# Row statistics of the late output projection: sums with the additions, squares and one normalising instruction on ScalarE, and the next phase's sums one unit ahead

## The chip, the cores and the metric

The kernel runs on one core of one Trainium2 chip. The metric is device time in microseconds (us) for one execution of the whole program, all four layers. One core has TensorE (PE, matmuls, with a separate record PEld for loading the stationary operand), VectorE (DVE), ScalarE (ACT), GpSimd (POOL) and SyncE (SP), which here issues every DMA. Each engine works through its own queue in order, so an instruction that waits holds up everything behind it on that engine.

## The reference

Four layers on an activation of 2048 rows by 640 columns, fp32. Layers 1 and 3 are attention over a sliding window of 256 with 32 heads of 20 columns; layers 2 and 4 are a Fourier mixing, written as products with DFT matrices. Each has a layer norm in front and a residual around it.

```python
x = x + _A_ref(_layernorm(x), A_wqkv, A_wo)
x = x + _B_ref(_layernorm(x), seq_re, seq_im, hid_re, hid_im)
x = x + _A_ref(_layernorm(x), A_wqkv, A_wo)
x = x + _B_ref(_layernorm(x), seq_re, seq_im, hid_re, hid_im)

def _layernorm(x, eps=1e-5):
    m = mean(x); v = var(x)
    return (x - m) / sqrt(v + eps)
```

`_A_ref` ends with a product by `wo` (the output projection). `_B_ref` is Re(DFT over the sequence of (DFT over the columns of x)). The change touches the place where these meet: the end of the output projection, its residual addition, the layer norm of the Fourier layer, and the beginning of the DFT over the sequence. This place occurs twice, in layers 1 to 2 and in layers 3 to 4. It is called the seam below, the first and the second.

## The kernel before

**Products.** fp32 operands are split into a high and a low part (`split`: the high part is a ScalarE copy, L156, the low part a subtraction on VectorE or GpSimd, L162), and a product is three matmuls (L169, L1139).

**Output projection.** The 640 columns that enter it are five chunks of 128. Three are multiplied early, during the heads; `late` multiplies the last two and adds the result to the early part, in 16 row blocks `t` of 128 rows. A row block is two halves of 320 columns with six matmuls each (L169), and each half ends in an addition on VectorE out of PSUM (L888) into the tile `xw`. After the heads these halves alternate between two PSUM banks, 5 and 6. The four sets of rows need their operands loaded and multiplied first (`load_o`, L741 on VectorE).

**Late rows, as they are now.** After the second addition VectorE takes the statistics of the row (`stats`: two BATCH_NORM_STATS, L183, an aggregate, L185, and the addition of epsilon, L187) and the negative mean (L894). The rest is posted: `post(d, f)` runs `f` after `d` ticks, and a tick passes for every `PACE` = 0.65 of accounted work (`spend`: 0.147 for a matmul of `late`, 2.7 for a unit a1, 1.4 for a2, 2.0 for b7). In ticks after the row's end: at 3 the power -0.5 on GpSimd (L896); at 5 the store of the row; at 6 two ScalarE instructions, x minus mean (L857) and times the power (L858). Rows of the first half (t below 8) are split at 8. Rows of the second half belong to row t-8: at 8 their columns 384 to 640 are added to those of row t-8 on GpSimd (`sum1`, L951), at 10 that sum is split. The last two rows take another way (`norm_last`, `norm_rest`): power at 1, VectorE normalises columns 384 to 640 (L869), adds (L951) and at 3 splits; the other columns follow at 8 on ScalarE (L876, L877).

**The DFT over the sequence** is a list of units (`take_fourier`): a1 for j = 0 to 7, a2 for j = 0 to 5, then b7 0, a2 6, b7 1, a2 7, b7 2, b5 0 to 2, b 3 to 7, and g 0 to 7. A unit (`seq`) loads matrices ahead (`load_to`, L1049), forms sums and differences of them and splits them (`cut_to`; L1062 on GpSimd, L1070 on VectorE), prepares its row operand (`x_to`) and then multiplies. While rows are left, `after_heads` runs about one unit after each row, and `unit` starts a2 j only when the split of row j+9 has been issued, a2 6 and a2 7 only after that of row 15.

**Row operands of the b units** (`x_to`): `xb3_to` splits a difference that GpSimd made (`sum3`, L955), `xb4_to` first calls `sum4_to`, two VectorE additions (L963, L964), and splits their result, and `parts` splits 128 columns of the row (the tile `rr`), which the unit's first matmuls read.

Of the kernel before, what the change touches and what calls it, by code (L numbers as in the profile page):

```python
# [15 lines left out]
P = 128  # L16
S = 2048
D = 640
# [5 lines left out]
NB = S // P  # L24
# [3 lines left out]
EPS = 1e-5  # L28
# [32 lines left out]
class Net:  # L61
# [114 lines left out]
            pass  # L176


    def stats(self, x, root=True):
        nc = self.nc  # L180
        st = self.ln.tile([P, 2, 6], F32, name="st", tag="st")
        for i in range(2):
            nc.vector.bn_stats(out=st[:, i, :], in_=x[:, i * 320:(i + 1) * 320])  # L183
        mv = self.ln.tile([P, 2], F32, name="mv", tag="mv")
        nc.vector.bn_aggr(out=mv, in_=st)  # L185
        rs = self.ln.tile([P, 2], F32, name="rs", tag="rs")
        nc.vector.tensor_scalar_add(rs[:, 0:1], mv[:, 1:2], EPS)  # L187
        if not root:
            return mv, rs
# [660 lines left out]
    def late(self, xsrc, xdst, hook):  # L850
        nc = self.nc
        ks = range(EARLY, KC)
        w = dict(zip(ks, self.late_w))

        def norm(t, xw, st, nm):
            xn = self.y_part(t)
            nc.scalar.activation(xn, xw, AF.Identity, bias=nm, scale=1.0)  # L857
            nc.scalar.activation(xn, xn, AF.Copy, scale=st[1][:, 1:2])  # L858
            if t < NB // 2:
                self.post(2, lambda: self.split_x(t, 0, 384))  # L860
            else:
                j = t - NB // 2
                self.post(2, lambda: self.sum1(j, nc.gpsimd))
                self.post(4, lambda: self.split_x(j, 384, 640))

        def norm_last(t, xw, st):

            xn, j = self.y_part(t), t - NB // 2
            nc.vector.tensor_scalar(out=xn[:, 384:], in0=xw[:, 384:], scalar1=st[0][:, 0:1], scalar2=st[1][:, 1:2],  # L869
                                    op0=OP.subtract, op1=OP.mult)  # L870
            self.sum1(j, nc.vector)
            self.post(1, lambda: self.split_x(j, 384, 640, nc.vector))

        def norm_rest(t, xw, st, nm):
            xn = self.y_part(t)
            nc.scalar.activation(xn[:, :384], xw[:, :384], AF.Identity, bias=nm, scale=1.0)  # L876
            nc.scalar.activation(xn[:, :384], xn[:, :384], AF.Copy, scale=st[1][:, 1:2])  # L877

        for t in range(NB):
            sb, i = t // 4, t % 4  # L880
            y = self.y_part(t)
            xw = self.raw()
            for hf in range(2):
# [4 lines left out]
                nc.vector.tensor_tensor(out=xw[:, cs], in0=p, in1=y[:, cs], op=OP.add)  # L888
                if hf == 0:
                    yield 1  # L890
            self.post(5, lambda t=t, xw=xw: nc.sync.dma_start(xdst[t * P:(t + 1) * P, :], xw))
            st = self.stats(xw, False)
            nm = self.ln.tile([P, 1], F32, name="nm", tag="nm")
            nc.vector.tensor_scalar_mul(nm, st[0][:, 0:1], -1.0)  # L894
            fast = t >= NB - 2
            self.post(1 if fast else 3, lambda st=st: nc.gpsimd.tensor_tensor(  # L896
                out=st[1][:, 1:2], in0=st[1][:, 0:1], in1=self.half, op=OP.pow))
            if NB // 2 - 1 <= t < NB - 1:
                self.post(4, lambda t=t: self.sum3(t - NB // 2 + 1))
            if fast:  # L900
                self.post(2, lambda t=t, xw=xw, st=st: norm_last(t, xw, st))
                self.post(8, lambda t=t, xw=xw, st=st, nm=nm: norm_rest(t, xw, st, nm))
            else:
                self.post(6, lambda t=t, xw=xw, st=st, nm=nm: norm(t, xw, st, nm))
            hook(t)
            self.late_t = t + 1
            yield 1
# [178 lines left out]
    def x_to(self, n):  # L1086
        nc = self.nc
        while self.n_x <= min(n, len(self.order) - 1):
            u = self.n_x
            self.n_x += 1  # L1090
            ph, j = self.order[u][2:]
            a, b = self.y_part(j), self.y_part(j + NB // 2)
            first = self.order[u][:2] == (0, 0)

            x = [self.xa[j]]
            if ph in ("b", "b7"):
                x = [self.xb[j], self.xm[j % 2]]
# [347 lines left out]
```

## Time and profile before

| | |
|---|---|
| median of 3 runs | 2337.34 us (2332.91 to 2339.71) |
| profiled execution, its own time | 2337.11 us |
| its span, first to last instruction | 2335.4 us |
| PE busy | 2245.9 us (96%) |
| DVE busy | 1576.0 us (67%) |
| ACT busy | 1110.4 us (48%) |
| POOL busy | 1010.4 us (43%) |

A span is the time from the first to the last instruction. Busy shares are averages over stages that have different limits; the two seams lie at about 574 to 700 us and 1733 to 1858 us, and the prediction reads them stage by stage. In rows of groups the figures are count, busy us, mean ns of one, then the engine's idle time in front of them and what ended it. In rows of waits they are total us, times, longest us. In rows of the timeline they are start, duration, engine, line, operation, and in brackets the idle time in front and its releaser. In rows of stages each engine has its busy us and number of instructions, and PEclk is the granted clock of TensorE as a share of full speed.

### The profile page before, as it was taken

The page shows a single profiled execution, that of the slowest core. Times are in us where ns is not written, and L with a number is a line of the kernel's source. Part 1 is how long each engine was busy: PE and PEld are TensorE (multiplying, and loading weights), DVE is VectorE, ACT ScalarE, POOL GpSimd, SP SyncE. Part 2 cuts the span into 40 slices and gives each one's busy share as a digit, 9 for nine tenths or more (in the row PEclk, how much of TensorE's full clock was granted, in tenths as well). Part 3 has the DMA queues.
Part 4 walks back from the last instruction along what each step waited for, and adds up shares of the span by engine and source line. Part 5 has one row for each costly group of instructions (what it writes and reads, how often), then busy time and mean ns, then how long its engine had stood idle before and what let it go on. Part 6 is the DMA issues. An engine that isn't in the chain of part 4 may idle for free.

```text
span 2335.4 us, 40458 instructions
## 1 busy us (share of the span) xinstructions
PE 2245.9 (96%) x13584; PEld 1679.5 (72%) x13584; DVE 1576.0 (67%) x3781; ACT 1110.4 (48%) x1875; POOL 1010.4 (43%) x1506
## 2 busy tenths in 40 slices
PE   8999999999979999999999999999998899999999
PEld 7964444456758888889999554445667688888899
DVE  6357677675888888872451677776758888788622
ACT  3125555655645555541331355556566555456310
POOL 3036665776845132340120466557677332242300
PEclk9999999999999999999999999999999899999999
DMA  5545555674535454655455455557735353536453
GB/s 190 172 133 170 169 166 162 207 210 143 190 101 163 140 175 142 213 174 165 162 163 178 138 167 164 159 182 207 213 127 183 104 167 131 185 123 229 162 165 101
DMA packets 217264, 385.02 MB, mean 165 GB/s; under 512 B 38880, under 2 KB 85472, under 8 KB 217056
## 3 DMA queue, kind: packets, MB, share of 16 engines
q1 hardware_dynamic: 217056, 382.43, 51.9%
q8 instruction: 108, 1.77, 0.3%
q14 instruction: 100, 0.82, 0.1%
HBM read 267.39 MB, written 113.77 MB: 163 GB/s over the span
## 4 chain that ended last, share of the span: by engine, by line
PE 39%; ACT 3%; POOL 3%; DVE 3%; DMA 1%; issue 1%; SPq 0%; ACTq 0%; POOLq 0%; DVEq 0%
PE banks L169 17%; PE banks L1139 13%; PE banks L524 4%; PE banks L562 3%; ACT pt L532 2%; PE banks L495 2%; POOL big L162 0%; POOL x L741 0%; DMA pt<-c 0%; POOL ou L1073 0%; DVE rr L162 0%; POOL pt L538 0%; PE banks L238 0%; ACT qp L156 0%; POOL kp L162 0%
## 5 line engine op out<-in xcount | busy, mean ns | idle before, releaser
L500 DVE CUSTOM_DVE_ANT_0 ux<-banks,mask 128x384 bf16<-128x384 f32 (+2 forms) x1024 | 545.0, 532 | 231.4 <-PE banks L495 127.9
L532 ACT ACTIVATE pt<-banks 128x768 f32<-128x768 f32 (+2 forms) x512 | 394.5, 771 | 350.4 <-PE banks L524 238.7
L169 PE MATMUL banks<-big,wc 128*128 128x512 f32 x1200 | 351.2, 418 | 2.3 <-ACT x L418 2.3
L538 POOL TENSOR_SCALAR_AFFINE_SELECT pt<-pt 128x256 f32<-128x256 f32 x512 | 212.0, 415 | 298.4 <-ACT pt L532 283.6
L524 PEld LDWEIGHTS banks<-qp,kp 61*128 61x128 f32 x1024 | 100.6, 183 | 249.1 <-ACT pt L532 214.0
L169 PEld LDWEIGHTS banks<-big,wc 128*128 128x128 f32 x1200 | 207.1, 189 | 78.7 <-issue 40.7
L524 PE MATMUL banks<-qp,kp 61*128 61x384 f32 (+2 forms) x1024 | 227.0, 430 | 29.7 <-ACT pt L532 23.1
L562 PE MATMUL banks<-pt,vq 128*32 128x384 f32 (+2 forms) x2816 | 208.7, 393 | 0.0
L162 DVE TENSOR_TENSOR qp<-pt,qp 128x512 fp32r<-128x512 f32 (+2 forms) x223 | 185.4, 851 | 31.1 <-ACT qp L156 29.3
L156 ACT ACTIVATE qp<-pt 128x512 fp32r<-128x512 f32 (+2 forms) x223 | 134.0, 619 | 144.2 <-POOL pt L1062 41.7
L495 PE MATMUL banks<-kp,qp 60*128 60x384 f32 (+2 forms) x1024 | 188.7, 340 | 4.0 <-DVE mc L500 4.0
L542 POOL TENSOR_SCALAR_AFFINE_SELECT pt<-pt 128x256 f32<-128x256 f32 x448 | 184.1, 411 | 0.0
L1073 POOL TENSOR_TENSOR pt<-pt,pt 128x512 f32<-128x512 f32 x40 | 66.5, 1666 | 225.4 <-DMA pt<-c 145.9
L162 DVE TENSOR_TENSOR c<-pt,c 128x512 fp32r<-128x512 f32 x184 | 151.2, 837 | 6.3 <-ACT c L156 5.1
L1326 DVE TENSOR_TENSOR x<-banks,x 128x320 f32<-128x320 f32 x64 | 29.8, 488 | 179.9 <-DMA x<-x_d 88.3
L156 ACT ACTIVATE c<-pt 128x512 fp32r<-128x512 f32 x184 | 113.8, 627 | 74.3 <-DVE pt L1074 22.1
L1139 PE MATMUL banks<-qp,big 128*128 128x512 f32 x600 | 143.1, 390 | 1.2 <-DVE qp L162 1.2
L1139 PEld LDWEIGHTS banks<-qp,big 128*128 128x128 f32 x600 | 111.9, 188 | 24.8 <-DVE qp L162 2.1
L1139 PE MATMUL banks<-c,big 128*128 128x512 f32 x444 | 113.8, 402 | 12.0 <-ACT big L156 9.8
L495 PEld LDWEIGHTS banks<-kp,qp 60*128 60x128 f32 x1024 | 109.3, 187 | 22.2 <-DVE mc L500 11.6
L1139 PE MATMUL banks<-qp,xc 128*128 128x512 f32 x480 | 117.9, 394 | 5.0 <-DVE xc L162 2.9
L169 PE MATMUL banks<-big,pt 128*128 128x320 f32 x768 | 118.2, 309 | 0.8 <-DVE pt L1263 0.8
(192 smaller groups left out, 4268.0 us busy)
## 6 DMA issues: line engine op xcount, KB each, us to landing
pt<-c SPq DMA_DIRECT2D x184, 512.0 KB
qk_d<-c SPq DMA_DIRECT2D x80, 512.0 KB
kp<-qk_d SPq DMA_DIRECT2D x384, 80.0 KB
qp<-qk_d SPq DMA_DIRECT2D x384, 80.0 KB
kp<-u_d SPq DMA_DIRECT2D x32, 640.0 KB
o_d<-ou SPq DMA_DIRECT2D x64, 256.0 KB
x_d<-x SPq DMA_DIRECT2D x48, 320.0 KB
v_d<-pt SPq DMA_DIRECT2D x16, 768.0 KB
```

The source lines that it names most:

```text
L156: nc.scalar.activation(hi, src, AF.Copy, scale=-1.0 if neg else 1.0)
L162: (eng or nc.vector).tensor_tensor(out=lo, in0=src, in1=hi.bitcast(F32), op=OP.subtract)
L169: self.nc.tensor.matmul(p, x, y, start=n == 0, stop=n == last)
L495: nc.tensor.matmul(p, qp[quad % 2][b:b + 60, z, qb * P:(qb + 1) * P], kp[quad % 2][b:b + 60, z, k0 * P:(qb + 1) * P], start=True, stop=True)
L500: nc.vector.tensor_tensor_reduce(out=self.ux[:, :n * P], in0=p, in1=self.mask[:, 384 - n * P:], scale=1.0, scalar=NEG, op0=OP.add, op1=OP.max,
L524: nc.tensor.matmul(p, kp[quad % 2][b:b + 61, z, kb * P:(kb + 1) * P], qp[quad % 2][b:b + 61, z, kb * P:(kb + n) * P], start=True, stop=True)
L532: nc.scalar.activation(pt[quad, kb][:, 2 * z:2 * z + 2, :n * P], self.banks[:, 0:2, :n * P], AF.Exp, scale=SCALE)
L538: nc.gpsimd.affine_select(out=t[:, :, 0:P], in_=t[:, :, 0:P], pattern=[[0, 2], [1, P]], compare_op=OP.is_ge, fill=0.0, base=0, channel_mul ...
L542: nc.gpsimd.affine_select(out=t[:, :, 256:384], in_=t[:, :, 256:384], pattern=[[0, 2], [-1, P]], compare_op=OP.is_gt, fill=0.0, base=0, ch ...
L562: nc.tensor.matmul(acc[quad, bk][32 * h:32 * h + 32, (qb - 4 * bk) * P:(e - 4 * bk) * P], vq[:, 96 * (kb % 4) + 21 * h:96 * (kb % 4) + 21 ...
L1073: nc.gpsimd.tensor_tensor(out=t1, in0=p, in1=t1, op=OP.subtract)
L1139: nc.tensor.matmul(self.banks[:, bk, :], p, b[q], start=start and m == 0, stop=stop and last and m == 2, skip_group_check=True)
```

## The change

- `stats` loses its `root` argument; `late` no longer calls it.
- The addition of each half becomes a VectorE `tensor_tensor_reduce` that also sums the row; the second half starts from the first half's sum. One VectorE instruction makes minus the mean.
- At tick 1 ScalarE squares x minus mean over the 640 columns with an accumulated sum (its element output goes to `y_part(t)`, which is overwritten later). At tick 3 VectorE makes variance plus epsilon and GpSimd the power. At tick 5 ScalarE makes minus mean times the power for the 128 rows, one column, and normalises with scale and bias in one instruction.
- Rows of the first half are normalised whole and split at tick 7. Rows of the second half: columns 384 to 640 at tick 5, `sum1` at 6, the split and the columns 0 to 384 at 7. All rows take this way; `norm_last` and `norm_rest` are gone. For rows 13 to 15 `sum1` and the low part of the split are on VectorE, for rows 8 to 12 on GpSimd.
- In `x_to`, the split of the 128 columns goes ahead of `xb3_to` and `xb4_to`, and after `xb4_to(j + 1)` comes `sum4_to(j + 2)`, so that the sums for a unit are issued one unit before their split.

```diff
@@ late @@
-        def norm(t, xw, st, nm):
-            xn = self.y_part(t)
-            nc.scalar.activation(xn, xw, AF.Identity, bias=nm, scale=1.0)
-            nc.scalar.activation(xn, xn, AF.Copy, scale=st[1][:, 1:2])
...
+        def squares(t, xw, st):
+            nc.scalar.activation(self.y_part(t), xw, AF.Square, bias=st[:, 2:3], scale=1.0, accum_out=st[:, 3:4])
+        def power(st):
+            nc.vector.tensor_scalar(out=st[:, 4:5], in0=st[:, 3:4], scalar1=1.0 / D, scalar2=EPS,
+                                    op0=OP.mult, op1=OP.add)
+            nc.gpsimd.tensor_tensor(out=st[:, 5:6], in0=st[:, 4:5], in1=self.half, op=OP.pow)
+        def norm(t, xw, st):
+            nc.scalar.activation(st[:, 6:7], st[:, 2:3], AF.Copy, scale=st[:, 5:6])
             if t < NB // 2:
+                norm_cols(t, xw, st, 0, 640)
                 self.post(2, lambda: self.split_x(t, 0, 384))
+                return
+            j, eng = t - NB // 2, nc.vector if t >= NB - 3 else nc.gpsimd
+            norm_cols(t, xw, st, 384, 640)
+            self.post(1, lambda: self.sum1(j, eng))
+            self.post(2, lambda: self.split_x(j, 384, 640, eng))
+            self.post(2, lambda: norm_cols(t, xw, st, 0, 384))
+        def norm_cols(t, xw, st, a, b):
+            nc.scalar.activation(self.y_part(t)[:, a:b], xw[:, a:b], AF.Identity, bias=st[:, 6:7], scale=st[:, 5:6])
...
-                nc.vector.tensor_tensor(out=xw[:, cs], in0=p, in1=y[:, cs], op=OP.add)
+                nc.vector.tensor_tensor_reduce(
+                    out=xw[:, cs], in0=p, in1=y[:, cs], scale=1.0, scalar=st[:, 0:1] if hf else 0.0,
+                    op0=OP.add, op1=OP.add, accum_out=st[:, hf:hf + 1])
...
-            st = self.stats(xw, False)
-            nc.vector.tensor_scalar_mul(nm, st[0][:, 0:1], -1.0)
...
+            nc.vector.tensor_scalar_mul(st[:, 2:3], st[:, 1:2], -1.0 / D)
+            self.post(1, lambda t=t, xw=xw, st=st: squares(t, xw, st))
+            self.post(3, lambda st=st: power(st))
+            self.post(5, lambda t=t, xw=xw, st=st: norm(t, xw, st))
...
@@ x_to @@
                 x = [self.xb[j], self.xm[j % 2]]
+                self.parts(x[1], b[:, 256:384], 0)
                 if first:
                     self.xb3_to(j + 1)
-                if ph == "b":
+                if ph == "b" and first:
                     self.xb4_to(j + 1)
-                self.parts(x[1], b[:, 256:384], 0)
+                    self.sum4_to(j + 2)
             if ph == "b5":
                 x = [self.xb[j]]
                 self.xb4_to(j + 1)
+                self.sum4_to(j + 2)
```

More of the change, by code (lines that the diff above doesn't have):

```diff
@@ L176, in all3, with stats @@
             pass
-    def stats(self, x, root=True):
+    def stats(self, x):
         nc = self.nc
@@ L187, in stats @@
         nc.vector.tensor_scalar_add(rs[:, 0:1], mv[:, 1:2], EPS)
-        if not root:
-            return mv, rs
         nc.gpsimd.tensor_tensor(out=rs[:, 1:2], in0=rs[:, 0:1], in1=self.half, op=OP.pow)
@@ L853, in late @@
         w = dict(zip(ks, self.late_w))
-        def norm(t, xw, st, nm):
-            xn = self.y_part(t)
-            nc.scalar.activation(xn, xw, AF.Identity, bias=nm, scale=1.0)
-            nc.scalar.activation(xn, xn, AF.Copy, scale=st[1][:, 1:2])
+        def squares(t, xw, st):
[6 more added lines that the diff above has]
+            nc.scalar.activation(st[:, 6:7], st[:, 2:3], AF.Copy, scale=st[:, 5:6])
             if t < NB // 2:
+                norm_cols(t, xw, st, 0, 640)
                 self.post(2, lambda: self.split_x(t, 0, 384))
[L861 to L877, printed above, removed]
+                return
[6 more added lines that the diff above has]
+            nc.scalar.activation(self.y_part(t)[:, a:b], xw[:, a:b], AF.Identity, bias=st[:, 6:7], scale=st[:, 5:6])
         for t in range(NB):
@@ L882, in late @@
             xw = self.raw()
+            st = self.ln.tile([P, 8], F32, name="ls", tag="ls")
             for hf in range(2):
@@ L891, in late @@
             self.post(5, lambda t=t, xw=xw: nc.sync.dma_start(xdst[t * P:(t + 1) * P, :], xw))
-            st = self.stats(xw, False)
[L893 to L897, printed above, removed]
+            nc.vector.tensor_scalar_mul(st[:, 2:3], st[:, 1:2], -1.0 / D)
+            self.post(1, lambda t=t, xw=xw, st=st: squares(t, xw, st))
+            self.post(3, lambda st=st: power(st))
+            self.post(5, lambda t=t, xw=xw, st=st: norm(t, xw, st))
             if NB // 2 - 1 <= t < NB - 1:
                 self.post(4, lambda t=t: self.sum3(t - NB // 2 + 1))
[L900 to L904, printed above, removed]
             hook(t)
```

## The prediction

> **What bounds the kernel now.** The page first: one execution, and TensorE almost always busy.
>
> ```profile
> span 2335.4 us, 40458 instructions
> PE 2245.9 (96%) x13584; PEld 1679.5 (72%) x13584; DVE 1576.0 (67%) x3781; ACT 1110.4 (48%) x1875; POOL 1010.4 (43%) x1506
> ```
>
> The execution took 2337.11 us, 0.23 below the median; I sum against it. TensorE leaves 2335.4 - 2245.9 = 89.5 us in all, so the change can win only where TensorE waits near the late rows. Next the stages of both seams (us from A to B, then busy us and count of PE, PEld, DVE, ACT, POOL, then PEclk, DMA), then TensorE's waits from 597 to 701 and from 1755 to 1858.
>
> ```profile
> 574.00:597.00 23.00, 22.60 (x167) 17.05 (x159) 16.91 (x54) 18.65 (x31) 21.18 (x30) 1.00 0.56 171
> 597.00:624.40 27.40, 21.98 (x107) 18.40 (x107) 25.94 (x34) 16.52 (x28) 25.86 (x21) 0.96 0.67 215
> 624.40:647.00 22.60, 22.52 (x114) 20.26 (x114) 17.61 (x49) 14.29 (x23) 17.07 (x23) 0.90 0.38 135
> 647.00:664.00 17.00, 11.72 (x39) 8.06 (x40) 13.31 (x27) 10.00 (x22) 3.83 (x5) 0.80 0.36 114
> 672.00:695.00 23.00, 20.75 (x75) 14.60 (x75) 18.39 (x27) 9.62 (x24) 10.66 (x12) 0.93 0.33 106
> ```
>
> ```profile
> PE banks L1139 <- ACT big L156: 4.9, 1, 4.9
> PE banks L169 <- DVE x L888: 4.4, 1, 4.4
> PE banks L1139 <- ACT rr L156: 3.9, 5, 1.6
> ...
> PE banks L1139 <- ACT big L156: 5.0, 1, 5.0
> PE banks L1139 <- ACT rr L156: 3.9, 5, 1.6
> PE banks L169 <- DVE x L888: 2.3, 1, 2.3
> ```
>
> Three waits per seam: for the additions of row 9 (L888; row 10 needs their banks), for the split of row 13 (ACT big), and for the 128-column splits of the b units (ACT rr). Together 13.2 us in the first seam and 11.2 in the second. VectorE is the crowded engine (25.94 of 27.40 us before the first wait); ScalarE has room (16.52). From 624.4 to 647 TensorE does not wait.
>
> **The change, part by part.** First what a row costs on each engine.
>
> ```profile
> L888 DVE TENSOR_TENSOR x<-banks,big 128x320 f32<-128x320 f32 x64 | 29.9, 483 | 18.2 <-PE banks L169 18.1
> L183 DVE BATCH_NORM_STATS2 st<-x 128x6 f32<-128x320 f32 x80 | 35.0, 479 | 8.0 <-DMA x<-x 8.0
> L185 DVE BATCH_NORM_AGGREGATE mv<-st 128x2 f32<-128x12 f32 x64 | 13.4, 209 | 2.6
> L500 DVE CUSTOM_DVE_ANT_0 ux<-banks,mask 128x384 bf16<-128x384 f32 x896 | 499.3, 557 | 185.8 <-PE banks L495 102.0 <-DVE mc L500 1.5
> L500 DVE CUSTOM_DVE_ANT_0 ux<-banks,mask 128x256 bf16<-128x256 f32 x64 | 27.2, 425 | 27.3 <-PE banks L495 12.3 <-PE banks L524 10.4
> L500 DVE DVE_READ_ACCUMULATOR2_ANT mc<- 128x1 f32 x1024 | 84.9, 83 | 0.0
> L857 ACT ACTIVATE big<-x,nm 128x640 f32<-128x640 f32 x28 | 23.0, 820 | 1.1 <-DVE nm L894 1.0
> L858 ACT ACTIVATE big<-big,rs 128x640 f32<-128x640 f32 x28 | 23.3, 831 | 6.9 <-POOL rs L896 5.5
> L876 ACT ACTIVATE big<-x,nm x4: 602/603/604, 651.7 to 1814.5; 128x384 f32<-128x384 f32 x4
> ```
>
> VectorE, per row. L500 is the same operation as the new addition: 320 columns lie midway between 256 (425 ns) and 384 (557), so 491, and 83 for the read of its sum: 574 ns against 483. Two halves cost 0.18 us more. Two L183 and one L185 go: 2 x 0.479 + 0.209 = 1.167. The epsilon addition and the minus mean are replaced by one instruction each of the same shape, so nothing. Net -0.985 us; the second half's wait for the first half's sum is not shown (0 to 0.1; I take 0, since L500 waited 1.5 us in 896). Over 16 rows 15.8 us per seam.
>
> ScalarE, per row. The square stands in L857's place. Of L858, Identity takes the place, with a second pointer (not shown: 0 to the 0.28 below; I take 0.1, since bias and scale differ by 0.011). From 640 columns (820) and 384 (603), 0.848 ns a column and 0.28 us fixed. The one-column copy adds 0.28; reading the sum 0 to 0.28, 0.08 by VectorE's read. Rows 8 to 15 are normalised in two pieces: 0.28 and another pointer more. So 0.46 for an early and 0.84 for a late row, 8 x 0.46 + 8 x 0.84 = 10.4 us per seam. The Trainium skill ("ScalarE: Activation LUTs", What ACT_TABLE_LOAD costs) has 93 ns for each pointer, which no row here isolates; by it the late row would be 0.83, and the sum the same. Rows 10 to 15 lie in the third stage: 14.29 + 6 x 0.84 = 19.3 of 22.60 us, still under TensorE's 22.52. I charge 0.5 us per seam for queueing there, from 0 to 4. In the first stage, rows 0 to 6, ScalarE is at 18.65 of 23.00 and gets 7 x 0.46 = 3.2: nearly full. I take 0, since TensorE stands still for row 9 soon after, for reasons of VectorE and a DMA, and a delay of up to that wait ends there; without that cover it costs up to 3.2.
>
> GpSimd keeps its power; `sum1` and a low part move to VectorE for row 13 too (rows 14, 15 had them there), while L869 (below) leaves. On SP the stores stay at tick 5 and the matrix loads keep their place in the order: no DMA is added.
>
> The new wait: VectorE's variance now waits for the square, with the next row's additions queued behind it, and TensorE's banks behind those. Cover: the variance is issued after the next unit's split on VectorE (0.68 us in row 650.06's form below), while square and read take about 0.9. Without cover it costs up to 0.9 a row, until two banks (a row of matmuls) are used up.
>
> *Row 9's additions.*
>
> ```profile
> 616.97 1.15 ACT L156 ACTIVATE c<-pt 128x512 fp32r<-128x512 f32 x2 [2.60 <-DMA pt<-c]
> 620.55 3.43 DVE L162 TENSOR_TENSOR c<-pt,c 128x512 fp32r<-128x512 f32 x2
> 624.44 3.57 PE L169 MATMUL banks<-qp,kp 128*128 128x320 f32 x12 [4.42 <-DVE x L888]
> 631.09 1.92 PE L169 MATMUL banks<-qp,kp 128*128 128x320 f32 x12
> 1777.18 1.16 ACT L156 ACTIVATE c<-pt 128x512 fp32r<-128x512 f32 x2 [5.10 <-DMA pt<-c]
> 1777.86 3.31 DVE L162 TENSOR_TENSOR c<-pt,c 128x512 fp32r<-128x512 f32 x2
> ```
>
> In the first seam VectorE's backlog holds the split at 620.55, though its high part was there 3 us earlier. Rows 7 and 8 save 2 x 0.985 = 2.0 us of it. A shorter stall also slows the clock less: the 12 matmuls behind it took 3.57 against 1.92; I take 0.5 of that 1.65. In the second seam the split follows its ScalarE part within 0.7 us, and that waited 5.10 us for a DMA; earlier VectorE work meets the same landing, so 0. Ends: 0 to 6.1 and 0 to 2.3.
>
> *Behind row 15.*
>
> ```profile
> 645.46 0.82 DVE L869 TENSOR_SCALAR big<-x,mv,rs 128x256 f32<-128x256 f32 x1 [0.45 <-POOL rs L896]
> 647.98 0.88 DVE L888 TENSOR_TENSOR x<-banks,big 128x320 f32<-128x320 f32 x2
> 650.06 0.68 DVE L1070 TENSOR_TENSOR pt<-pt 128x512 f32<-128x512 f32 x1
> 650.84 0.63 ACT L156 ACTIVATE c<-pt 128x512 fp32r<-128x512 f32 x1 [2.72 <-DVE pt L1070]
> 651.83 3.08 PE L1139 MATMUL banks<-c,big 128*128 128x512 f32 x6 [4.87 <-ACT big L156]
> 655.20 1.46 PE L1139 MATMUL banks<-c,rr 128*128 128x512 f32 x3 [0.29 <-ACT rr L156]
> ```
>
> Row 14's special way (L869) holds row 15's additions; their statistics hold L1070; ScalarE waits for that, and row 13's split, at its tick 10, stands behind it. After: row 13's split is at tick 7. A row with an a2 unit is (12 x 0.147 + 1.4)/0.65 = 4.9 ticks, so it comes before row 15's end, 9.7 ticks on. The unit at 651.83 then starts when TensorE is free, at about 647, with no stall. What is late next is b7 0 (655.20): its 128-column split comes behind, on ScalarE, a matrix split after L1070 (0.6), row 14's copy and 256 columns (0.9), the square of row 15 (0.9), a split (0.4) and 384 columns (0.7), then itself and its low part (1.0): 4.5 us after an L1070 that can run at about 647.1. So 651.6 instead of 655.20: gain 3.6 in each seam. Ends: 0, the wait moved whole, and 4.87 plus the slow clock (3.08 against about 1.55): 6.4.
>
> *The b units.*
>
> ```profile
> 684.30 0.96 DVE L963 TENSOR_TENSOR big<-big 128x256 f32<-128x256 f32 x1
> 685.29 0.43 DVE L964 TENSOR_TENSOR kp<-big,big 128x256 f32<-128x256 f32 x1
> 686.40 0.73 DVE L162 TENSOR_TENSOR rr<-big,rr 128x128 fp32r<-128x128 f32 x1 [0.68 <-ACT rr L156]
> 691.15 0.73 DVE L162 TENSOR_TENSOR rr<-big,rr 128x128 fp32r<-128x128 f32 x1 [0.68 <-ACT rr L156]
> ```
>
> A unit lasts 691.15 - 686.40 = 4.75 us: the sums, ScalarE's split of them, then its rr split, then VectorE again after 0.68 idle. With rr first and the sums already made, VectorE never waits there: 5 x 0.68 = 3.4, the last unit without sums a little more, less 0.4 for the sums now first in a busier stretch: 3.0 per seam, of the 3.9 that TensorE waits (ends 0 and 3.9). A rule speaks against it: "SBUF — State Buffer" of the Trainium skill (Who interferes with whom) says that a VectorE instruction with two SBUF inputs contends with GpSimd's reads. L963 at 0.96 beside L964 at 0.43, both of 256 columns, agrees; by it L964 could also take 0.96, 0.5 us a unit, and the gain would be 0.5.
>
> Sum: first seam 2.0 + 0.5 + 3.6 + 3.0 - 0.5 = 8.6; second 0 + 3.6 + 3.0 - 0.5 = 6.1. 2337.1 - 14.7 = 2322.4 us; I say 2322. Behind the seams TensorE is busy without gaps, so what is won there stays.
>
> **The rivals.**
>
> *More goes.* All named waits vanish, 13.2 + 11.2, and with them the slow clock behind two of them, 1.65 + 1.53 a seam: 30.8 us, 2306. For: each hangs on VectorE. Against: the DMA in the second seam, and ScalarE's list behind row 15.
>
> *It is hidden or given back.* Behind row 15 the wait moves whole to b7 0, and GpSimd's contention keeps the b units at 4.75 us. What is left is 2.5 - 1.0: 2336. For: L963 at 0.96.
>
> *Slower: VectorE waits for ScalarE.* The variance waits for a square that stands behind ScalarE's other work, and additions and banks wait with it. With ScalarE one row behind (about 2.4 us of work), VectorE waits 1.7 us a row and saves 0.985: 0.7 x 13 rows x 2 = 18 us, no gain elsewhere: 2355. It decides from 0.985 us of wait a row on. Against: 19.3 of 22.60.
>
> *Slower by tables.*
>
> ```profile
> L156 ACT ACT_TABLE_LOAD x1 | 1.3, 1283 | 0.8 <-PEq L1435 0.8
> ```
>
> One load in the whole run, with Exp, Copy and Identity. If Square needed another table, rows 0 to 4 would pay two loads each among the exponentials: 2 x 1.283 x 5 x 2 = 26 us, at most 2348 with the gain. "ScalarE: Activation LUTs" of the Trainium skill (Table sets: the hidden batching unit) lists the cheap functions of every set without Square; no run shows it.
>
> **How the numbers follow.** Forecast 0.52 (its own range 2313 to 2329), more 0.15, given back 0.17, VectorE waiting 0.13, tables 0.03. A measurement of this kernel tells about 0.3%, 7 us, from no change: faster 0.67, same 0.17, slower 0.16. The range, 2304 to 2341, leaves out the far part of the slow cases and a little of the first rival.
>
> **What would show it.** VectorE's busy time falls by about 30 us, ScalarE's rises by about 20. TensorE's wait for the row 9 additions falls to about 2.4 us in the first seam and stays in the second; its wait for ACT big goes and one of about 3 for ACT rr at b7 0 comes; a b unit takes about 4.1 us. Wrong, if VectorE shows waits for ScalarE's accumulated sum of more than a microsecond in total per row, if table loads appear, or if 624 to 647 grows by more than 1 us.

## The result and the profile after

The changed kernel took 2348.60 us (median, 2344.69 to 2350.96) against 2337.34 us (2332.81 to 2340.64) for the kernel before, timed beside it. The ratio is 1.0051, with a 95% interval of 1.0037 to 1.0064: about 12 us slower, where 2322 was forecast.

The page of the changed kernel, its span and its busy time:

```profile
span 2344.5 us, 40514 instructions
PE 2244.3 (96%) x13584; PEld 1678.0 (72%) x13584; DVE 1557.6 (66%) x3749; ACT 1128.1 (48%) x1955; POOL 1003.4 (43%) x1502
```

The span is 9.1 us longer, although VectorE has 18.4 us less to do, ScalarE only 17.7 us more at 48%, and TensorE the same work. So no engine was overfilled; somebody waits. TensorE's waits in the first seam (total us, times, longest):

```profile
PE banks L169 <- DVE ls L887: 6.8, 4, 2.6
PE banks L1135 <- ACT rr L156: 3.7, 1, 3.7
PE banks L1135 <- ACT xc L156: 2.4, 1, 2.4
PE banks L1135 <- DVE rr L162: 1.6, 4, 0.5
PE banks L1135 <- ACT big L156: 1.3, 1, 1.3
```

The wait for a row's additions (L887, in place of L888) came once before, with 4.4 us behind row 9. Now it comes four times: 2.6 behind row 9, and three more further on. The same stretch by stage, as before:

```profile
597.00:624.40 27.40, 24.96 (x118) 20.02 (x116) 24.29 (x35) 19.24 (x41) 24.70 (x20) 1.00 0.74 237
624.40:647.00 22.60, 16.79 (x83) 14.65 (x84) 10.93 (x34) 13.55 (x30) 14.01 (x18) 0.92 0.31 105
```

In the second line, rows 10 to 15, TensorE fell from 22.52 busy us of 22.60 to 16.79. VectorE (17.61 to 10.93), ScalarE (14.29 to 13.55) and GpSimd (17.07 to 14.01) also did less than before in the same time. Most of VectorE's fall is the statistics that it no longer takes. ScalarE has the squares to do in addition and still stands idle a little longer. That all engines idle more points to a chain that goes through all of them.

The next table, worked out from the starts of the matmul rows in TensorE's timelines, gives us for each part of a seam (first / second): from the first late row to the first unit, from row 10 to row 15, from row 15 to b7 0, from b7 0 to the first g unit.

| kernel | to first unit | rows 10 to 15 | row 15 to b7 0 | b7 0 to g |
|---|---|---|---|---|
| before | 19.1 / 19.1 | 19.2 / 18.8 | 11.6 / 11.6 | 41.0 / 41.0 |
| after | 20.7 / 23.5 | 23.7 / 23.7 | 10.2 / 10.1 | 39.0 / 39.1 |

Rows 10 to 15 lose 4.5 and 4.9 us, the rows among the heads 1.6 and 4.4. The end of the rows gains 1.4 and 1.5, the b units 2.0 and 1.9. The stretch between first unit and row 10 gains 0.3 and 0.1, and the start of the g units takes 1.0 more in the first seam and 1.1 less in the second. Together +3.4 and +4.7; the rest of the 9.1 lies outside the seams, 0.8 of it ahead of the first.

**The ring.** The timeline of the changed kernel between the matmuls of row 11 (632.68) and row 12 (638.16) (start, duration, engine, line, operation, idle before and its releaser):

```profile
632.34 0.29 ACT L863 ACTIVATE ls<-ls 128x1 f32<-128x1 f32 x1 [0.85 <-POOL ls L860]
632.66 0.60 ACT L875 ACTIVATE big<-x,ls 128x256 f32<-128x256 f32 x1
633.34 0.74 POOL L945 TENSOR_TENSOR big<-big,big 128x256 f32<-128x256 f32 x1 [0.33 <-ACT big L875]
634.12 0.42 ACT L156 ACTIVATE big<-big 128x256 fp32r<-128x256 f32 x1 [0.85 <-POOL big L945]
634.44 0.70 ACT L875 ACTIVATE big<-x,ls 128x384 f32<-128x384 f32 x1
635.04 0.62 ACT L156 ACTIVATE qp<-pt 128x512 fp32r<-128x512 f32 x1
635.76 0.69 DVE L162 TENSOR_TENSOR qp<-pt,qp 128x512 fp32r<-128x512 f32 x1 [2.73 <-ACT qp L156]
636.51 0.82 ACT L855 ACTIVATE big<-x,ls 128x640 f32<-128x640 f32 x1
637.46 0.15 DVE L858 TENSOR_SCALAR ls<-ls 128x1 f32<-128x1 f32 x1 [1.01 <-ACT big L855]
637.61 0.49 DVE L887 CUSTOM_DVE_ANT_0 x<-banks,big 128x320 f32<-128x320 f32 x1
637.69 0.55 POOL L860 TENSOR_TENSOR ls<-ls,half 128x1 f32<-128x1 f32 x1 [2.33 <-DVE ls L858]
638.16 2.02 PE L169 MATMUL banks<-qp,kp 128*128 128x320 f32 x12 [2.17 <-DVE ls L887]
638.28 0.29 ACT L863 ACTIVATE ls<-ls 128x1 f32<-128x1 f32 x1 [0.85 <-POOL ls L860]
```

Read it downwards; each bracket names the line that the engine had waited for. ScalarE normalises row 9 (632.66), GpSimd adds (L945), ScalarE splits the sum, normalises the other columns and only then makes the high part of the next unit's matrix (635.04). VectorE has stood idle for 2.73 us for it before it makes the low part (635.76). Behind that low part on VectorE stands row 10's variance (L858); here it waits 1.01 us more, for row 10's square, which stands on ScalarE behind the same matrix. Behind the variance stand row 11's additions, and for these TensorE waits before row 12 (638.16). The power of row 10 (637.69) waited 2.33 us for the variance, ScalarE's copy (638.28) waits for the power, and behind the copy stands everything with which the next turn begins. One turn takes 638.28 - 632.34 = 5.94 us here, from row 9's copy to row 10's. The next take 4.98, 3.93 and 3.92 (copies at 643.26, 647.19 and 651.11). Before, TensorE took 3.14 us for a row and its unit, as from row 11 (631.09, in the prediction) to row 12:

```profile
634.23 1.92 PE L169 MATMUL banks<-qp,kp 128*128 128x320 f32 x12
```

**The heads.** In the second seam, ScalarE and TensorE among the last exponentials:

```profile
1743.51 0.83 ACT L855 ACTIVATE big<-x,ls 128x640 f32<-128x640 f32 x1 [1.85 <-DVE ls L893]
1744.34 0.58 ACT L530 ACTIVATE pt<-banks 128x512 f32<-128x512 f32 x1
1744.97 0.39 PE L522 MATMUL banks<-qp,kp 61*128 61x256 f32 x2 [1.60 <-ACT pt L530]
```

Row 0's square waits 1.85 us for its mean on VectorE, the exponential stands behind it, and TensorE waits 1.60 for that.

### The profile page after: what moved, and what is told of

It reads as the page before. It is cut to its first block, busy times and chain, and to the rows that moved or that the text cites. A ratio compares the mean times of both kernels' runs of the same rounds, so it can differ in the third digit from the quotient of the medians.

```text
span 2344.5 us, 40514 instructions
## 1 busy us (share of the span) xinstructions
PE 2244.3 (96%) x13584; PEld 1678.0 (72%) x13584; DVE 1557.6 (66%) x3749; ACT 1128.1 (48%) x1955; POOL 1003.4 (43%) x1502
## 4 chain that ended last, share of the span: by engine, by line
PE 38%; ACT 4%; DVE 3%; POOL 3%; issue 2%; DMA 1%; SPq 0%; ACTq 0%; POOLq 0%; DVEq 0%
PE banks L169 17%; PE banks L1135 13%; PE banks L522 4%; PE banks L560 3%; ACT pt L530 2%; PE banks L493 2%; DVE qp L162 1%; POOL x L739 0%; POOL pt L540 0%; ACT qp L156 0%; POOL ou L1067 0%; POOL pt L536 0%; DMA rr<-r_d 0%; ACT big L875 0%; POOL big L162 0%
## 5 line engine op out<-in xcount | busy, mean ns | idle before, releaser
L162 DVE TENSOR_TENSOR qp<-pt,qp 128x512 fp32r<-128x512 f32 (+2 forms) x223 | 187.8, 862 | 43.2 <-ACT qp L156 41.5
L162 DVE TENSOR_TENSOR c<-pt,c 128x512 fp32r<-128x512 f32 x184 | 151.6, 838 | 11.4 <-ACT c L156 10.1
L1322 DVE TENSOR_TENSOR x<-banks,x 128x320 f32<-128x320 f32 x64 | 29.9, 489 | 182.1 <-DMA x<-x_d 94.6
L169 PEld LDWEIGHTS banks<-big,pt 128*128 128x128 f32 x768 | 114.0, 188 | 3.5 <-ACT pt L1256 2.1
```

What stands on the lines that cost most here:

```text
L162: (eng or nc.vector).tensor_tensor(out=lo, in0=src, in1=hi.bitcast(F32), op=OP.subtract)
L169: self.nc.tensor.matmul(p, x, y, start=n == 0, stop=n == last)
```

## The experiments

Two theories at the start. *Ring*: rows 10 to 15 are slow because the variance at tick 3 stands on VectorE behind the next unit's split, which on ScalarE stands behind the previous row's normalising; only the order matters. *Load*: ScalarE's added work, above all the square, is too much. A third, that the additions with their sums are themselves too long, stood beside them. Line numbers move by a few between kernels. Each kernel was timed beside the kernel before, whose median was 2336 to 2338 us; the ratios are compared, and a difference of two ratios is turned into time with 2337.

### The b units alone

```diff
 (kernel before, x_to)
+                self.parts(x[1], b[:, 256:384], 0)
                 if first:
                     self.xb3_to(j + 1)
-                if ph == "b":
+                if ph == "b" and first:
                     self.xb4_to(j + 1)
-                self.parts(x[1], b[:, 256:384], 0)
+                    self.sum4_to(j + 2)
...
                 self.xb4_to(j + 1)
+                self.sum4_to(j + 2)
```

> The kernel before with the part on the b units alone (split of the 128 columns first, sums one unit ahead). All theories agree that it wins; the sizes differ. By the prediction's step, 3.0 us in each seam: 2337.3 - 6.0 = 2331. By the trace of the changed kernel the wait for ACT rr is gone (3.9 us a seam) but the wait of the first g unit for ACT xc grows from 1.05 to 2.4: 2.5 a seam, 2332. If the gain of the b units belonged to the delayed rows and not to this part, no change: 2337.

Measured 2330.98 us, ratio 0.9976 [0.9964, 0.9988]: 5.6 us faster. From b7 0 to the first g unit it takes 38.1 in both seams, 2.9 less than before, as the prediction's 3.0 had it. Two units in TensorE's timeline:

```profile
677.01 0.61 PE L1141 MATMUL banks<-qp,rr 128*128 128x512 f32 x2
678.05 0.50 PE L1141 MATMUL banks<-qp,rr 128*128 128x512 f32 x1 [0.42 <-DVE rr L162]
...
681.13 0.61 PE L1141 MATMUL banks<-qp,rr 128*128 128x512 f32 x2
```

A unit takes 4.12 us, where it was 4.75. This part wins on its own.

### VectorE's statistics back

```diff
 (changed kernel, late)
-                nc.vector.tensor_tensor_reduce(out=xw[:, cs], in0=p, in1=y[:, cs], ...
+                nc.vector.tensor_tensor(out=xw[:, cs], in0=p, in1=y[:, cs], op=OP.add)
...
-            nc.vector.tensor_scalar_mul(st[:, 2:3], st[:, 1:2], -1.0 / D)
-            self.post(1, lambda ...: squares(t, xw, st))
-            self.post(3, lambda ...: power(st))
+            mv, rs = self.stats(xw, False)
+            nc.vector.tensor_scalar_mul(st[:, 2:3], mv[:, 0:1], -1.0)
+            self.post(3, lambda ...: nc.gpsimd.tensor_tensor(
+                out=st[:, 5:6], in0=rs[:, 0:1], in1=self.half, op=OP.pow))
```

> The changed kernel, but with the plain additions and VectorE's row statistics of before; the one normalising instruction on ScalarE, its ticks, the common way of rows 13 to 15 and the part on the b units stay. Round trip theory (ScalarE, VectorE, GpSimd, ScalarE in turn, each in its own order, make every row late): the waits for additions in rows 11 to 15 go, as do those among the heads, and with the b units and the end of the rows as changed the time is 2326 to 2332. Load theory (ScalarE's added work is too much): the square, 1.0 us a row, is gone too, so also below 2337. Rival that VectorE was the bound and its 0.985 us a row matter: the row 9 wait comes back and rows 10 to 15 stall more, 2345 or above.

Measured 2330.05 us, ratio 0.9977 [0.9968, 0.9986]. Rows 10 to 15 take 18.3 and 20.0. So the sums and the square cost some 17 us together (1.0051 against 0.9977), although VectorE is busy some 0.8 us a row longer without them (worked out under Prices below). That VectorE bounds these rows is refuted. One instruction for the normalising and the common way of rows 13 to 15 bring nothing beyond the b units' gain.

### The square without a reader, and without the square

```diff
 (changed kernel, power)
-            nc.vector.tensor_scalar(out=st[:, 4:5], in0=st[:, 3:4], scalar1=1.0 / D, scalar2=EPS,
+            nc.vector.tensor_scalar(out=st[:, 4:5], in0=st[:, 2:3], scalar1=0.0, scalar2=1.0,
 (the second kernel also)
-            self.post(1, lambda t=t, xw=xw, st=st: squares(t, xw, st))
```

> The changed kernel with the square on ScalarE kept, but VectorE makes a constant 1.0 in place of variance plus epsilon, from the minus mean, so it no longer waits for ScalarE's accumulated sum (the rows are not scaled to unit variance: that part of the computation is left out). Round trip theory: TensorE's waits for L887 in rows 11 to 15 (4.2 us a seam) mostly go, the heads' waits for ScalarE's exponentials stay: 2338 to 2342. Load theory: ScalarE's work is the same, so 2348 as the changed kernel.

> As the kernel with the unread square, and the square itself left out as well (so no variance is computed at all; that part of the computation is left out). ScalarE has 1.0 us a row less than in the changed kernel. Round trip theory: the heads' waits for the exponentials go too, since nothing on ScalarE waits for a row's mean at tick 1 any more: 2328 to 2334, some 8 below the unread square. Load theory: the whole loss goes here and not before, 16 us a seam of ScalarE work: 2330, and the step from the unread square is 15 or more. If the sum taken with the additions were itself the cause (longer additions, later banks), it stays near 2345.

Measured 2342.22 us, ratio 1.0026 [1.0015, 1.0037], and 2336.90 us, ratio 1.0006 [0.9997, 1.0014]. Against 1.0051 the direct wait for the accumulated sum is worth 5.8 us and the square itself 4.7 more, each give or take 3 to 4 us by the intervals. Rows 10 to 15 take 22.1 us in both seams with the unread square, so most of the 4.7 lies elsewhere; 2.4 of it stands behind row 15 (10.3 against 9.1 in each seam). The load theory fails on the first number: the same work, a quarter of a per cent less time. But the ring theory in its simple form fails on the second. Without any square the time should have fallen to about 2330, and rows 10 to 15 still take 21.5 and 21.6. The view of waits from 624 to 652 of the kernel without the square says why:

```profile
DVE qp L162 <- ACT qp L156: 7.7, 4, 2.8
ACT big L156 <- POOL big L944: 6.4, 5, 4.0
POOL ls L860 <- DVE ls L858: 5.6, 4, 2.0
...
ACT ls L863 <- POOL ls L860: 5.0, 5, 1.5
```

VectorE waits for ScalarE's matrix split, GpSimd's power for the one-column instruction on VectorE, ScalarE's copy for the power. The ring is closed without the square. What closes it is the place of L858, behind the low part of the split.

### One instruction moved, to open the ring

The same kernel as the last, and the one-column instruction is issued at the row's end.

```diff
             nc.vector.tensor_scalar_mul(st[:, 2:3], st[:, 1:2], -1.0 / D)
+            nc.vector.tensor_scalar(out=st[:, 4:5], in0=st[:, 2:3], scalar1=0.0, scalar2=1.0, ...)
             self.post(3, lambda st=st: power(st))
 (and the same instruction taken out of power)
```

> As the kernel without the square (2336.9; no variance is computed, that part of the computation is left out), but the one-column instruction that stands for the variance is issued at the row's end on VectorE and not at tick 3, behind the next unit's matrix split. Not one instruction more or less. Ring theory: GpSimd's power no longer waits for VectorE's matrix split, the ring is open, TensorE's waits for L887 in rows 11 to 15 go: 2328 or less. If the sum taken with the additions is what costs (longer, a wait between the halves), no change: 2337.

Measured 2327.69 us, ratio 0.9971 [0.9960, 0.9982]: 8 us from the place of one instruction of 0.15 us. Rows 10 to 15 take 18.7 and 19.8. TensorE's rows after the wait behind row 9:

```profile
624.70 3.35 PE L169 MATMUL banks<-qp,kp 128*128 128x320 f32 x12 [3.24 <-DVE ls L885]
630.86 1.92 PE L169 MATMUL banks<-qp,kp 128*128 128x320 f32 x12
634.00 1.92 PE L169 MATMUL banks<-qp,kp 128*128 128x320 f32 x12
637.14 1.92 PE L169 MATMUL banks<-qp,kp 128*128 128x320 f32 x12
```

They follow each other every 3.14 us again. The sums in the additions are still there, so they do not cost it.

### The same instruction moved the other way

The kernel with VectorE's statistics, and the addition of epsilon goes from the row's end to tick 3.

```diff
 (stats) 
+        if not root:
+            return mv, rs
         nc.vector.tensor_scalar_add(rs[:, 0:1], mv[:, 1:2], EPS)
-        if not root:
-            return mv, rs
 (late)
-            self.post(3, lambda ...: nc.gpsimd.tensor_tensor(out=st[:, 5:6], in0=rs[:, 0:1], ...
+            self.post(3, lambda st=st, mv=mv: power_eps(st, mv))   # epsilon, then the power
```

> The run with VectorE's statistics (2330, the whole of the computation), with one instruction moved: the addition of epsilon, one column, 0.15 us, goes from the row's end to tick 3, ahead of the power, and so behind the next unit's matrix split on VectorE. Ring theory: this closes the ring again, without square and without sums in the additions; TensorE's waits for the additions of rows 11 to 15 come back, some 3 to 4.5 us a seam: 2336 to 2339. If the ring needs the longer additions or the square, no change: 2330.

Measured 2340.10 us, ratio 1.0007 [0.9998, 1.0015], against 0.9977: 7 us slower. Rows 10 to 15 go from 18.3 and 20.0 to 21.7 and 21.6, with TensorE's waits back behind rows 11 and 12:

```profile
638.17 2.02 PE L169 MATMUL banks<-qp,kp 128*128 128x320 f32 x12 [0.83 <-DVE x L893]
...
642.96 2.02 PE L169 MATMUL banks<-qp,kp 128*128 128x320 f32 x12 [1.38 <-DVE x L893]
```

Neither the square nor the sums are in this kernel. The place of one VectorE instruction opens and closes the ring in both directions.

### The variance on GpSimd

```diff
 (changed kernel, power)
-            nc.vector.tensor_scalar(out=st[:, 4:5], in0=st[:, 3:4], scalar1=1.0 / D, scalar2=EPS,
+            nc.gpsimd.tensor_scalar(out=st[:, 4:5], in0=st[:, 3:4], scalar1=1.0 / D, scalar2=EPS,
```

> The changed kernel with the variance and epsilon instruction moved from VectorE to GpSimd, ahead of the power, so that nothing on VectorE waits for the square any more. If the loss were VectorE's wait for ScalarE's sum alone, the time falls at least to that of the unread square, 2342. Ring theory: a row's normalising is one ring, from the unit's matrix split on ScalarE and VectorE over the variance, the power on GpSimd, the copy, the normalising, the sum on GpSimd and the split on ScalarE to the next unit's matrix split. The ring is only closed elsewhere (square, GpSimd, copy and the rest on ScalarE, about 1.0 + 0.9 + 0.3 + 0.6 + 0.85 + 0.4 + 0.7 + 0.6 = 5.4 us against a row of 3.15 on TensorE), so it stays near 2348.

Measured 2347.43 us, ratio 1.0056 [1.0043, 1.0069]: no gain. Rows 10 to 15 take 24.7, so the turn is about as long without VectorE's variance in it, through the square on ScalarE. That VectorE's direct wait for ScalarE's sum is the whole matter is refuted. So the place of the variance on VectorE is one way in which the ring closes, and the square on ScalarE, which stands behind the same matrix split, is another.

### The normalising later

```diff
 (changed kernel, late)
-            self.post(5, lambda t=t, xw=xw, st=st: norm(t, xw, st))
+            self.post(8, lambda t=t, xw=xw, st=st: norm(t, xw, st))
```

> The changed kernel with the normalising at tick 8 instead of 5 (sum at 9, split at 10, which is the tick of the split before the change); the square and the power stay at 1 and 3. Ring theory: ScalarE's copy now comes behind the next row's square and the next unit's matrix split, so the power is ready when ScalarE gets to it and the ring spans two rows: the waits for L887 in rows 11 to 15 shrink by half or more, 2340 or less. Load theory: the work is the same, 2348.

Measured 2335.01 us, ratio 0.9999 [0.9990, 1.0007]: 12 us less than the changed kernel, with the same instructions. Rows 10 to 15 take 18.8 and 19.3. From ScalarE's timeline, the squares of rows 10 and 11 (L855):

```profile
631.66 0.81 ACT L855 ACTIVATE big<-x,ls 128x640 f32<-128x640 f32 x1
...
632.61 0.42 ACT L156 ACTIVATE big<-big 128x256 fp32r<-128x256 f32 x1
...
633.54 0.61 ACT L156 ACTIVATE qp<-pt 128x512 fp32r<-128x512 f32 x1
634.06 0.28 ACT L863 ACTIVATE ls<-ls 128x1 f32<-128x1 f32 x1
634.37 0.60 ACT L875 ACTIVATE big<-x,ls 128x256 f32<-128x256 f32 x1
634.88 0.81 ACT L855 ACTIVATE big<-x,ls 128x640 f32<-128x640 f32 x1
```

Row 10's copy (L863) has no wait in front of it any more: between row 10's square and it, ScalarE splits row 9's sum (632.61) and makes the next unit's matrix (633.54), and by then the power is there. This is the answer to the load theory: from row 10 to row 15 ScalarE is busy 15.04 of 18.75 us (625.34 to 644.09), a larger share than the 15.90 of 23.69 in the changed kernel (626.49 to 650.18), and it does not delay TensorE there.

### Both ways, by rows

```diff
 (changed kernel, late)
+                if t < 7:      # plain addition
...
+            if t < 7:          # VectorE's statistics, power at 3
...
+            else:              # sums, square at 1, variance and power at 3
...
-            self.post(5, lambda t=t, xw=xw, st=st: norm(t, xw, st))
+            self.post(5 if t < 7 else 8, lambda t=t, xw=xw, st=st: norm(t, xw, st))
```

> A version meant to beat both kernels: rows 0 to 6, which run among the heads, have plain additions and VectorE's statistics (normalised at tick 5 by the one instruction); rows 7 to 15 have the sums and the square, normalised at tick 8; the part on the b units stays. If among the heads the square, which waits on ScalarE for the row's mean with exponentials behind it, costs TensorE the 1.6 us and 4.4 us by which the heads end later in the two seams, 2335 less these 6: 2329. If those delays are noise of the profiled run, no change: 2335.

Measured 2335.16 us, ratio 0.9990 [0.9981, 0.9998], against 0.9999 for the normalising later alone: 2 us, within the two intervals, where 6 were expected. The wait for the exponentials fell to 1.2 and 1.4 us a seam, from 2.3 and 2.8 in the changed kernel. But the stretch to the first unit takes 20.1 and 20.7, and 19.9 in both seams with the squares in it and the normalising late. The kernels with the unread square, with the variance on GpSimd and with the rows alone (below), which treat these rows nearly as the changed kernel does, take 20.4, 20.9 and 21.7, each in both seams. So the 4.4 us of the changed kernel's second seam were not a steady cost of the square among the heads: they stand in one profiled execution, and what part of the 12 us the heads carry stays open. Some 0.8 us a seam or more over the 19.1 of before remains in every kernel with the one normalising instruction, square or not.

### The rows alone

```diff
 (changed kernel: the diff of x_to undone)
```

> The changed kernel with the part on the b units undone, so the row part alone. If the two parts add up: 2348 + 5.4 = 2353 to 2354. If the rows' delay already hides part of the b units' waits, less: 2350.

Measured 2350.69 us, ratio 1.0058 [1.0046, 1.0071]. Against 1.0051 the b units' part brings about 1.6 us here, within the two intervals, and 5.6 alone. The parts do not add up in the medians, although in the profiles the stretch from b7 0 to the first g unit takes 42.6 and 42.3 without the part and 39.0 and 39.1 with it. Part of it is given back right behind: from the first g matmul on, 57 matmuls take 15.4 us in both seams without the part and 16.5 with it, 2.1 us together. What cancels the rest is open.

### Two more orders

```diff
 (with VectorE's statistics: seq)
-        self.cut_to(n + 1)
-        self.x_to(n + 1)
+        self.x_to(n + 1)
+        self.cut_to(n + 1)
```

> A version meant to beat both: VectorE's statistics and one normalising instruction as in the run with VectorE's statistics (2330), and in each unit the row operand is prepared ahead of the next unit's matrices, so that the split of the 128 columns and the first split of the g units do not stand behind a matrix split that waits for a difference on VectorE. If that order is what TensorE waits for there (ACT rr 4.6 and ACT xc 2.4 us a seam), 2 to 4 us a seam go: 2322 to 2326. If the matrices are then late instead, no change: 2330.

Measured 2331.36 us, ratio 0.9981 [0.9972, 0.9991], against 0.9977: no gain. The wait for ACT rr stays at 4.6 and that for ACT xc at 2.4.

```diff
 (both ways by rows: cut_to, phase g)
-                nc.gpsimd.tensor_tensor(out=t1, in0=p, in1=t1, op=OP.subtract)
+                eng = nc.vector if j == 0 and self.order[u][:2] == (0, 0) else nc.gpsimd
+                eng.tensor_tensor(out=t1, in0=p, in1=t1, op=OP.subtract)
```

> The two-way version, and the first matrix difference of the first g unit of the first part goes from GpSimd to VectorE. In the changed kernel VectorE stood idle for 2.57 us there until GpSimd had done it, behind its splits for the last b units, and TensorE waited 2.43 us for ACT xc. If that is what it waits for, 2 us a seam go: 4 less than the two-way version. If the matrices land no earlier or the splits take its place: no change.

Measured 2332.37 us, ratio 0.9976 [0.9965, 0.9986]: 3 us less than the two-way version. Of TensorE's waits in the first seam, the one for VectorE's low part in the first g unit is now:

```profile
PE banks L1149 <- DVE xc L162: 2.5, 1, 2.5
```

The wait for ACT xc fell from 2.4 to 0.4, and 1.4 of it came back as a longer wait for VectorE's low part (1.1 in the two-way version). This version, the b units alone and the kernel with VectorE's statistics beat the kernel before by about the same, 0.23 to 0.24%. Of them the b units alone is the smallest edit.

## Why the prediction was wrong

The forecast was 2322, the result 2348.60, with the sign wrong.

**The step that failed** is "Cover: the variance is issued after the next unit's split on VectorE (0.68 us in row 650.06's form below), while square and read take about 0.9. Without cover it costs up to 0.9 a row, until two banks (a row of matmuls) are used up." The split was taken as 0.68 us of work that hides a wait. It is itself an instruction that waits, 2.73 us in the rows above, for a high part on ScalarE; that stands behind the previous row's normalising, and that behind the power of the row before. I followed the variance to what waits behind it, but not the cover to what stands ahead of it. Moving that one instruction gave 8 us one way and 7 the other. With the charge "0.5 us per seam for queueing there, from 0 to 4", worked out from ScalarE's busy share (19.3 of 22.60), the same error was made in a second form: a share says nothing of a ring. The rows measured 4.5 and 4.9 us longer. Of the prediction's own signs of being wrong, one came, that 624 to 647 grows by more than 1 us. VectorE's waits for the accumulated sum came to 3.1 us over the 16 rows of the first seam, not to more than 1 us a row, and no table load was added.

**The rival** "VectorE waits for ScalarE" had the sign and the victim, TensorE's banks, and 2355 for 2348.60; it had 0.13. It too priced load, "ScalarE one row behind", and its direct wait (L858 for L855) is a single one of 1.01 us between 624 and 652. Cutting that dependency alone (the unread square) won 5.8 of the 12 us; with the dependency kept, a later normalising won them all. Its sign and its nearness to 2348.60 were in part luck.

**Rows among the heads.** "I take 0, since TensorE stands still for row 9 soon after" did not hold: the first unit came 1.6 and 4.4 later. Row 9's wait fell from 4.42 to 2.60, as forecast ("about 2.4"), and stayed in the second seam (2.4). But in the first seam TensorE gets from the first unit to row 9 only after 23.0 us, where it was 21.4, so that only 0.3 us of the shorter wait reached row 10. Two new waits of 0.54 each stand there; TensorE's waits from 596 to 627 us have them:

```profile
PE banks L169 <- DVE ls L887: 2.6, 1, 2.6
...
PE banks L169 <- POOL kp L162: 0.5, 1, 0.5
PE banks L1135 <- DVE qp L162: 0.5, 1, 0.5
```

**Behind row 15.** Forecast: the wait for ACT big goes, one of about 3 for ACT rr at b7 0 comes, gain 3.6. Measured: 1.3 and 3.7 are left, gain 1.4 and 1.5. The list of what is late next was right in kind. What failed is "an L1070 that can run at about 647.1", 3.4 us behind the start of row 15's matmuls. It started 6.39 behind it (L1064, 656.57), as late as before (650.06, 6.41): row 15's additions (655.26) stand on VectorE behind a matrix low part (653.41) that waited 2.38 us for ScalarE, and behind row 13's low part (654.92), which waited 0.42. That is the same step as above.

**The b units** were right: 4.1 forecast for a unit, 4.12 measured, 2.9 of 3.0 a seam when the part stands alone. In the changed kernel it is 2.0 and 1.9, and the wait of the first g unit for ACT xc, which the sum left out, grew from 1.1 to 2.4. The contention that the Trainium skill, in "SBUF — State Buffer" (Who interferes with whom), made a rival did not decide. From VectorE's timeline of the changed kernel:

```profile
685.34 0.83 DVE L162 TENSOR_TENSOR rr<-big,rr 128x128 fp32r<-128x128 f32 x1
...
687.07 0.42 DVE L958 TENSOR_TENSOR kp<-big,big 128x256 f32<-128x256 f32 x1
...
689.41 0.28 DVE L162 TENSOR_TENSOR rr<-big,rr 128x128 fp32r<-128x128 f32 x1
...
690.60 0.84 DVE L958 TENSOR_TENSOR kp<-big,big 128x256 f32<-128x256 f32 x1
```

GpSimd's subtractions run from 685.28 to 686.76 and from 689.41 to 691.17. Single additions do take twice as long beside GpSimd, as that rule has it, but TensorE does not wait for them. It does wait for the low part of the 128 columns (DVE rr, 1.6 us in the waits of the first seam). In four units of the first seam that subtraction starts 0.06 us behind GpSimd's, as at 685.34, and takes 0.82 or 0.83 us. In the last two b units it starts no later than GpSimd's, takes 0.28 and 0.29, and TensorE has no such wait. No run moves GpSimd's subtraction, so that the overlap causes this wait is likely and not shown.

**Prices.** Read in these rows of groups of the changed kernel (count, busy us, mean ns):

```profile
L887 DVE CUSTOM_DVE_ANT_0 x<-banks,big,ls 128x320 f32<-128x320 f32 x32 | 17.6, 550 | 10.4 <-PE banks L169 7.8
L887 DVE CUSTOM_DVE_ANT_0 x<-banks,big 128x320 f32<-128x320 f32 x32 | 15.6, 489 | 12.2 <-PE banks L169 11.8
L855 ACT ACTIVATION_READ_ACCUMULATOR big<-x,ls 128x1 f32 x32 | 6.0, 187 | 0.0
L875 ACT ACTIVATE big<-x,ls 128x640 f32<-128x640 f32 x16 | 14.8, 923 | 0.5
L863 ACT ACTIVATE ls<-ls 128x1 f32<-128x1 f32 x32 | 9.2, 289 | 21.4 <-POOL ls L860 21.4
```

The addition was taken as 491 ns and is 489 from a constant and 550 from the first half's sum. The normalising with two pointers was taken as 0.92 and is 923; the copy as 0.28 and is 289. Reading ScalarE's sum was taken as 0.08 and is 187 ns. ScalarE's busy time rose by 17.7 us ("about 20"). VectorE's fell by 18.4, not 30. The additions, their reads and the statistics account for a fall of 26.1 us over the 32 rows: 29.9 for L888, 28.0 of L183's 35.0 and 6.7 of L185's 13.4 went, 38.5 for L887 came. That is 0.8 a row and not 0.985; the prediction counted L183 by its 479 ns, where 35.0 us for 80 make 437 of busy time each. Other VectorE work took longer, for instance L162 qp<-ou, 16 times, from 681 to 901 ns on average; the median stayed at 680, and a few took up to 1777. There is one table load in the run, as before, so that rival is out.

**Behind the seams.** "TensorE is busy without gaps, so what is won there stays" did not hold to the microsecond: the start of the g units took 1.0 us more in the first seam and 1.1 less in the second (last section).

## What to carry to other kernels

When an instruction is offered as cover for a wait, look up what that cover itself waits for: follow each queue backwards until the chain ends, and if it comes back to the instruction you started from one row earlier, add up one turn and compare that with the period of the bottleneck. The busy shares did not show this ring; idle time that rose on all engines at once did. Opened at one place, it no longer delayed rows 10 to 15 here: with the one-column step issued at the row's end they took 18.7 and 19.8 us, with the consumer posted later 18.8 and 19.3, against 19.2 and 18.8 before the change.

## What was not expected of the hardware

Reading an accumulated sum on ScalarE takes 187 ns, on VectorE 82 (L887's reads, 64 times 82 ns). A VectorE addition whose sum starts from an SBUF value is 61 ns longer than from a constant (550 and 489). And the clock granted to TensorE behind waits of nearly the same size differs. From 695 to 703 us, where TensorE waits for the first g unit, kernel before and b units alone:

```profile
695.00:703.00 8.00, 5.24 (x20) 3.56 (x20) 8.00 (x12) 6.04 (x13) 2.27 (x2) 1.00 0.27 83
```

```profile
695.00:703.00 8.00, 6.34 (x15) 4.70 (x16) 8.00 (x14) 5.57 (x12) 1.28 (x1) 0.57 0.38 108
```

1.00 against 0.57, with waits of 1.05 and 1.44 in the one and 1.74 and 1.43 in the other; in the second seam both have 0.72 there (1850 to 1862). So the 57 matmuls from the first g matmul on took 15.5 and 17.6 us in the two seams of the same kernel before, and what is won ahead of it can be lost there, or more won, by about 2 us. No run here tells what decides it.
